# Tying the two readings of an attention bank to one engine, with corrected ScalarE costs and a new order, in a kernel whose order is planned

## The chip, the cores and the metric

The kernel runs on one core of a Trainium2 chip. The metric is device time in microseconds (us), the median of several executions.

Engines: PE is TensorE, ACT is ScalarE, DVE is VectorE, POOL is GpSimd, SP issues DMAs.

## The reference, cut to what matters

```python
x = A_x                                   # 2048 x 512, bf16
for _ in range(2):
    x = x + A(layernorm(x))               # linear attention, 32 heads of 16
    x = x + B(layernorm(x))               # gated MLP, 512 -> 1376 -> 512

def A(x):
    q, k, v = split_heads(x @ wqkv)
    phi = lambda t: concat(softmax(t @ w_phi), softmax(-(t @ w_phi)))
    kv, z = phi(k).T @ v, phi(k).sum(0)
    num, den = phi(q) @ kv, phi(q) @ z + 1e-6
    return merge_heads(num / den) @ wo
```

The kernel computes the attention quotient of 128 rows from three PSUM banks. Each bank holds numerators (here called N) and two denominator terms (DS) side by side.

## The kernel before

All work is recorded as a list of `Op`s. Each has an engine, a planned cost (how long it holds the engine, and how long until its result is ready), dependencies, buffers and a priority `due`. `plan()` is a list scheduler: it gives each engine, at each step, the waiting `Op` with the lowest `due`, and so fixes the order in which instructions are written. `DUE` holds one tuned number for each of the 2112 `Op`s. `PLACE` holds one bit for each `Op` that either of two engines could do.

The parts that the change touches:

```python
def act(n, sbuf=False):                    # planned ScalarE cost of n elements: (occupies, until ready)
    return (n / 1.2 + (275 if sbuf else 52), n / 1.2 + (385 if sbuf else 170))

def dve(n, rate=1, more=56):               # the same for VectorE
    t = n / rate / 0.96 + more
    return t, t + 98

def evac(eng, due, out_, in_, deps, takes, uses, name, cols=512):
    both = {"ACT": ("ACT", act(cols), lambda: nc.scalar.copy(...), False),
            "DVE": ("DVE", dve(cols), lambda: nc.vector.tensor_copy(...), False)}
    ...                                    # an Op with the other engine as alternative (alt)

def attend(l, t, due, eq, made, how):
    ...
    for k in range(3):
        ps = Buf(p_q)                      # one of three "q" banks
        ...                                # 3, 3 and 2 matmuls of 144 columns into it (L766)
        for out_, buf, lo, hi in ((ed, DS, DH, DH + 2), (en, N, 0, DH)):
            out_.append(evac("ACT", due, ...))      # two readings of the same bank
    ...                                    # DVE: m, den, reciprocal, w from DS; pr, o from N; projection

for o, w in zip([o for o in ops if o.alt], PLACE):
    if w == "1":
        o.swap()                           # to the other engine
order = arrange(ops)
...
for o in order:                            # in the plan's order; early gaps on TensorE get filler matmuls
    o.emit()
```

In `plan()` the two readings of a bank are independent: each needs only the matmuls. A bank is free when both have ended.

The softmax here doesn't subtract the row's maximum and nothing guards it: scores larger than these inputs give would overflow.

## Time and profile before

| | before |
|---|---|
| median time | 393.26 us on record; 392.62 us beside the kernel after |
| span in the trace | 390.9 us |
| PE busy | 382.7 us, 98% |
| matmuls | 2830 |
| split banks (N and DS on different engines) | 43 of 96 |

Busy time, first part of the page of before (time, share of the span, instructions):

```profile
PE 382.7 (98%) x2830; PEld 232.1 (59%) x2830; DVE 305.8 (78%) x783; ACT 223.0 (57%) x580; POOL 33.9 (9%) x36
```

98% is no measure of the room left, because matmuls overlap each other: one of 512 columns is on record as busy for 379 ns, and the next starts 216 ns after it. A busy PE may still be late. I therefore used the spacing of matmul starts. Its medians (216 ns for 512 columns, 109 for 256, 56 for 128, 62 for 144, and so on) come to 375.3 us over all matmuls. What lies above that is called **excess** below: 10.5 us.

Excess before, by stage: 4.64 us in the head (0 to 30 us), 0.05 in the rest of the key stage (to 58), 2.94 in the first attention stage (58 to 100), 0.06 to 243 us, 2.20 in the second attention stage (243 to 300), 0.58 after it. 3.37 us of it stands before attention matmuls.

The same stages in the windows view (busy us and number of instructions of each engine). DVE is nearly full (95%) in both attention stages:

```profile
core 0: us, PE busy (x) PEld busy (x) DVE busy (x) ACT busy (x) POOL busy (x), PEclk, DMA share, GB/s
...
58.00:100.00 42.00, 40.68 (x431) 31.26 (x430) 39.76 (x133) 30.79 (x91) 0.05 (x1) 1.00 0.20 39
100.00:243.00 143.00, 143.00 (x894) 80.05 (x893) 115.33 (x255) 74.55 (x186) 12.19 (x11) 1.00 0.16 32
243.00:300.00 57.00, 56.19 (x537) 39.83 (x535) 54.05 (x184) 37.61 (x109) 0.00 (x0) 1.00 0.24 49
```

From the waits view of before (who waited for whom: us in total, times, longest). L766 is the attention matmul, L596 an ACT copy, L597 a DVE copy:

```profile
PEld L766 <- issue: 2.7, 8, 0.6
...
ACT N L596 <- DVE DS L597: 1.2, 3, 0.5
...
ACT DS L596 <- DVE N L597: 1.0, 2, 0.6
...
DVE DS L597 <- ACT N L596: 0.8, 2, 0.6
...
PE q L766 <- ACT DS L596: 0.5, 1, 0.5
...
PE q L766 <- DVE DS L597: 0.4, 1, 0.4
...
PE q L766 <- DVE N L597: 0.3, 2, 0.2
```

N and DS do not use each other's data, and yet in this trace the second reading of a bank never starts before the first has ended (32 ns after it at the soonest) where the two are on different engines. The timeline of before shows how. A split bank (start us, duration us, engine, line): ACT reads DS from 291.62 to 291.82, and DVE starts on N at 291.86.

```profile
291.62 0.20 ACT L596 COPY DS<-q 128x48 f32<-128x48 f32 x1 [0.21 <-PE q L766]
291.86 0.56 DVE L597 CAST N<-q 128x384 bf16<-128x384 f32 x1
```

A bank that ACT reads twice: N starts at 107.94, before DS has ended.

```profile
107.86 0.19 ACT L596 COPY DS<-q 128x32 f32<-128x32 f32 x1 [0.95 <-PE q L766]
107.94 0.38 ACT L596 CAST N<-q 128x256 bf16<-128x256 f32 x1
```

Over all banks: the second reading of a split bank never starts sooner than 32 ns after the first has ended, and in 18 of 43 it starts within 50 ns of that end. In 27 of the 53 banks read by one engine, the second starts before the first has ended.

In this trace, a late matmul that takes a bank starts 51 to 54 ns after the last reading of that bank has ended, so each wait can be put down to its bank. ACT reads DS until 67.77 us:

```profile
67.54 0.23 ACT L596 COPY DS<-q 128x48 f32<-128x48 f32 x1
...
67.82 0.35 PE L766 MATMUL q<-R,Eq 128*128 128x144 bf16 x3 [0.51 <-ACT DS L596]
```

### The profile page before, as it was taken

The numbers are of one execution on the slowest core, as the hardware profiler recorded it, in microseconds if no ns is written. First come the engines' busy times: TensorE is split into PE (matmuls) and PEld (weight loads), VectorE is DVE, ScalarE is ACT, GpSimd is POOL, SyncE is SP. The second block draws the span as 40 slices with busy tenths as digits, with TensorE's granted clock in tenths as the row PEclk, the third lists the DMA queues.
The fourth block names the chain that finished last, engine by engine and source line by source line (L and its number), as shares of the span: only waits on it lengthen the run. The fifth ranks groups of instructions, "written<-read, shape, count | busy, mean of one in ns | idle before, by whom it ended". The sixth has DMA issues, their size and how long they took to land.

```text
span 390.9 us, 7625 instructions
## 1 busy us (share of the span) xinstructions
PE 382.7 (98%) x2830; PEld 232.1 (59%) x2830; DVE 305.8 (78%) x783; ACT 223.0 (57%) x580; POOL 33.9 (9%) x36
## 2 busy tenths in 40 slices
PE   8999998999999999999999999999999999999996
PEld 5455565878554644446676555586765445446865
DVE  6989979999998998649485797999999955333534
ACT  5999979746355535416726289985554350542311
POOL 0248420000100010204110100000000000000000
PEclk9999999999999999999999999999999999999999
DMA  8297540221431312020100100012242503101111
GB/s 246 71 217 208 152 138 1 48 58 35 81 70 40 56 27 55 18 43 17 27 15 20 27 3 1 2 32 59 55 88 68 82 15 82 27 0 49 32 31 42
DMA packets 60869, 22.83 MB, mean 58 GB/s; under 512 B 52672, under 2 KB 59808, under 8 KB 60832
## 3 DMA queue, kind: packets, MB, share of 16 engines
q1 hardware_dynamic: 60416, 21.95, 24.5%
q8 instruction: 22, 0.36, 0.4%
q10 hardware_dynamic: 416, 0.39, 0.4%
q14 instruction: 15, 0.12, 0.1%
HBM read 7.91 MB, written 2.10 MB: 26 GB/s over the span
## 4 chain that ended last, share of the span: by engine, by line
PE 74%; DVE 13%; ACT 7%; DMA 2%; issue 2%; SPq 1%; DVEq 0%; ACTq 0%
PE b L861 29%; PE b L894 18%; PE b L674 6%; PE b L680 6%; PE b L797 4%; PE q L711 3%; PE b L748 3%; ACT Eq L752 3%; ACT N L596 2%; PE b L837 2%; DVE pr L790 1%; PE q L766 1%; DVE N L597 1%; DVE X L801 1%; DMA xnTA<-xn 1%
## 5 line engine op out<-in xcount | busy, mean ns | idle before, releaser
L861 PE MATMUL b<-xnTB,wgu 128*128 128x128 bf16 (+2 forms) x1200 | 150.7, 279 | 0.0
L861 PEld LDWEIGHTS <-wgu 128*128 128x128 bf16 x1200 | 97.9, 98 | 43.0
L894 PE MATMUL b<-wd,hT 128*128 128x512 bf16 (+2 forms) x363 | 83.4, 373 | 0.0
L865 ACT ACTIVATE gu<-b 128x512 bf16<-128x512 f32 (+1 forms) x83 | 49.0, 594 | 51.7 <-PE b L861 46.9
L894 PEld LDWEIGHTS <-hT 128*128 128x128 bf16 (+1 forms) x363 | 34.4, 98 | 33.6
L869 DVE TENSOR_TENSOR hT<-gu 128x512 bf16<-128x512 bf16 (+1 forms) x83 | 34.3, 417 | 23.0 <-ACT gu L596 21.9
L694 POOL TENSOR_TENSOR phiK<-ek,sk 128x512 bf16<-128x512 bf16 x30 | 33.2, 1125 | 182.2 <-ACT sk L690 89.9
L596 ACT CAST gu<-b 128x512 bf16<-128x512 f32 (+1 forms) x55 | 32.3, 586 | 21.3 <-PE b L861 21.1
L685 DVE TENSOR_REDUCE sk<-ek 128x64 f32<-128x1024 bf16 x32 | 38.5, 1213 | 6.7 <-ACT ek L677 6.7
L677 ACT ACTIVATE ek<-b 128x512 bf16<-128x512 f32 x64 | 36.0, 610 | 10.3 <-PE b L674 10.0
L752 ACT ACTIVATE Eq<-b 128x512 bf16<-128x512 f32 x64 | 38.2, 659 | 2.4 <-PE b L748 2.4
L901 DVE SCALAR_TENSOR_TENSOR X<-b,rsB,X 128x512 bf16<-128x512 f32 (+1 forms) x33 | 23.8, 731 | 19.5 <-PE b L894 19.4
L596 ACT CAST N<-q 128x384 bf16<-128x384 f32 (+1 forms) x70 | 31.3, 487 | 8.3 <-PE q L766 4.3
L797 PE MATMUL b<-wo,oT 128*128 128x512 bf16 x128 | 32.7, 379 | 0.6 <-DMA oT<-o 0.4
L674 PE MATMUL b<-Wk,xnTA 128*128 128x512 bf16 x128 | 32.7, 379 | 0.1
L680 PE MATMUL b<-wv,xnTA 128*128 128x512 bf16 x128 | 32.4, 379 | 0.1
L748 PE MATMUL b<-xnTA,Wq 128*128 128x512 bf16 x128 | 31.7, 379 | 0.0
L766 PE MATMUL q<-R,Eq 128*128 128x144 bf16 x256 | 27.8, 226 | 1.5 <-ACT DS L596 0.5
L766 PEld LDWEIGHTS <-Eq 128*128 128x128 bf16 x256 | 20.2, 98 | 11.8 <-issue 2.7
L649 ACT ACTIVATE lnA<-mvA,eps 128x1 f32<-128x1 f32 x32 | 9.1, 307 | 28.9 <-DVE mvA L644 28.5
L597 DVE CAST gu<-b 128x512 bf16<-128x512 f32 (+1 forms) x28 | 18.6, 663 | 8.6 <-PE b L861 8.3
L694 DVE TENSOR_TENSOR phiK<-ek,sk 128x512 bf16<-128x512 bf16 x34 | 23.3, 717 | 1.4 <-ACT sk L690 1.2
(70 smaller groups left out, 413.3 us busy)
## 6 DMA issues: line engine op xcount, KB each, us to landing
out_dram<-X SPq DMA_DIRECT2D x15, 128.0 KB, 1.7
X<-in_A_x_dram SPq DMA_DIRECT2D x6, 256.0 KB, 3.7
wgu<-in_B_W_gate_dram SPq DMA_DIRECT2D x4, 344.0 KB, 4.2
wgu<-in_B_W_up_dram SPq DMA_DIRECT2D x4, 344.0 KB, 4.2
wd<-in_B_W_down_dram SPq DMA_DIRECT2D x5, 256.0 KB, 4.4
wv<-in_A_wqkv_dram SPq DMA_DIRECT2D x2, 256.0 KB, 4.4
wo<-in_A_wo_dram SPq DMA_DIRECT2D x4, 128.0 KB, 2.8
oT<-o SPq DMA_TRANSPOSE x28, 2.4
```

What stands on the lines that cost most here:

```text
L596: both = {"ACT": ("ACT", act(cols), lambda: nc.scalar.copy(out=out_(), in_=in_()), False), "DVE": ("DVE", dve(cols), lambda: nc.vector.ten ...
L674: k = op("PE", mm(4, 512), due, lambda: [nc.tensor.matmul(kp.t[:], lhsT=xnTA[c][:, b, cols], rhs=Wk2[:, b, :], start=(b == 0), stop=(b == ...
L680: v = op("PE", mm(4, 512), due_v, lambda: [nc.tensor.matmul(vp.t[:], lhsT=xnTA[c][:, b, cols], rhs=wv[:, b, :], start=(b == 0), stop=(b == ...
L685: a = op("DVE", SUM16, due, lambda: nc.vector.tensor_reduce(out=sk.t[:], in_=ek.t[:].rearrange("p s (h f) -> p (s h) f", f=DH), axis=AX.X, ...
L694: e.tensor_tensor(out=ph.t[:].rearrange("p s (h f) -> p (s h) f", f=DH)[:, lo:lo + n], in0=ek.t[:].rearrange("p s (h f) -> p (s h) f", f=D ...
L748: q = op("PE", mm(4, 512), due(c, b), lambda b=b, qp=qp: [nc.tensor.matmul(qp.t[:], lhsT=Wq2[:, m, b * P:(b + 1) * P], rhs=xnTA[c][:, m, : ...
L752: done.append(op("ACT", act(512), due(c, b), lambda b=b, s=s, qp=qp: nc.scalar.activation(out=Eq[c][:, b, s, :], in_=qp.t[:], func=AF.Exp, ...
L766: pe.append(op("PE", mm(len(groups), GE), due, lambda ps=ps, groups=groups: [nc.tensor.matmul(ps.t[:, n * GE:(n + 1) * GE], lhsT=Eq[c][:, ...
L797: a = op("PE", mm(4, 512), due + 3, lambda: [nc.tensor.matmul(yp.t[:], lhsT=oT.t[:, b, :], rhs=wo[:, b, :], start=(b == 0), stop=(b == NB ...
L861: nc.tensor.matmul(ps.t[:, q * W:(q + 1) * W], lhsT=wgu[:, s, b, g * P:(g + 1) * P], rhs=xT.t[:, b, 0:W], start=(b == 0), stop=(b == NB - 1))
L865: nc.scalar.activation(out=gu.t[:, 0, 0:cols], in_=gp.t[:, 0:cols], func=AF.Relu)
L894: nc.tensor.matmul(yp.t[:, 0:c1 - c0], lhsT=h.t[:m, f * W + i * P:f * W + (i + 1) * P], rhs=wd[:m, f, c0:c1], start=(f == 0), stop=(f == N ...
```

## The change

Its intent: a bank's two readings stay on one engine, so that neither has to wait for another engine's reading of the bank, as in the 43 split banks above (32 ns or more from end to start); ScalarE's planned costs follow the spacing of instruction ends in a trace; priorities and engine choices are annealed anew for that plan (searched by many small random changes, of which those are kept that make the plan end sooner).

```diff
     def swap(self):
+        if self.twin:
+            self.twin.swap()
 ...
-    return (n / 1.2 + (275 if sbuf else 52), n / 1.2 + (385 if sbuf else 170))
+    return (n / 1.2 + (275 if sbuf else 64), n / 1.2 + (385 if sbuf else 170))
 ...
-            a = op("ACT", (210, 310), due, ...Ln of the key sums
+            a = op("ACT", (150, 265), due, ...
-            a = op("ACT", (110, 220), due, ...Exp of the key sums
+            a = op("ACT", (145, 262), due, ...
 ...
-            for out_, buf, lo, hi in ((ed, DS, DH, DH + 2), (en, N, 0, DH)):
+            for out_, buf, lo, hi in ((en, N, 0, DH), (ed, DS, DH, DH + 2)):
 ...
+            ed[-1].twin = en[-1]
 ...
-    for o, w in zip([o for o in ops if o.alt], PLACE):
+    tied = {o.twin for o in ops if o.twin}
+    for o, w in zip([o for o in ops if o.alt and o not in tied], PLACE):
 ... (PLACE: 301 new bits for 397; DUE: 2112 new numbers)
```

## The prediction

> **What bounds the kernel.** TensorE. The page gives PE 98% busy at full clock. Busy hides waits, so I took the start-to-start spacing of the 2830 matmul records. The medians (216 ns for 512 columns, 109 for 256, 82 for 192, 62 for 144, 56 for 128) summed over all matmuls give 375.3 us of the 390.9 us span. The rest: 1.2 us before the first matmul, 10.5 us of excess spacing, 3.8 us after the last matmul starts. Of the excess, 4.6 us lies in the first 30 us (1.7 us is the warm-up matmuls' double spacing); 3.3 us lies before attention matmuls (L766) waiting for a "q" bank; the rest is mostly waits for transposed tiles. From 100 to 243 us there is practically none. DVE and ACT matter only where they release banks late.
>
> **What the change does.**
> 1. Each of 96 attention banks has two evacuations, N and DS; 43 banks are split between ACT and DVE. The second reading of a split bank never starts sooner than 32 ns after the first ends; in 18 of 43 it starts within 50 ns of it, with 3.0 us of engine idle time before those. In banks read by one engine, 27 of 53 second readings start before the first has ended. [...] The kernel's plan treats the two as independent, so a split bank comes free later than planned. The change leaves no split banks.
> 2. It corrects planned ScalarE costs. End-to-end spacing of back-to-back instructions: 488 ns for 512 elements (plan 479, now 491), 383 for 384 (372, now 384), 102 for 48 (92, now 104), 145 for both small Ln and Exp of the key sums (210 and 110, now 150 and 145).
> 3. The order is annealed anew. Counted from the built program: 9 phi products (717 ns each on DVE, 1125 on POOL) go to POOL; 10 more 512-wide gu copies (682 against 599 ns) go from ACT to DVE. TensorE's instructions are the same but for 14 filler matmuls instead of 11: +0.65 us in the first 15 us, partly in stalls.
>
> **On the critical path.** Only the excess spacing can shrink. The bank waits (3.3 us) should fall to about 1 us. Of the other waits after 50 us (2.3 us) perhaps a third goes; new ones will appear where the order puts attention between other blocks. Head: about zero, fillers included. Net about -2 us. Without any stall after the head the kernel would still be near 387.5 us, so over 2% (385.4) is out of reach.
>
> **Prediction:** 391.2 us, 8 in 10 between 389.2 and 393.2. Faster by over 2%: 0.02; within 2%: 0.95; slower by over 2%: 0.03.
>
> **What would show it.** Excess spacing falls from 10.5 to about 8.5 us, mostly in 58 to 100 us and 243 to 300 us; attention-bank waits fall under 1.5 us; in the waits view no ACT N or DS behind a DVE reading, or the reverse; DVE's phi count is 25, POOL's 39.
>
> **What would make it wrong.** One engine for both readings may lengthen a bank's hold where that engine has a backlog; DVE is full from 60 to 160 and 250 to 310 us. POOL's phi products [...] may lengthen DVE instructions. A head 2 us longer would eat the gain..

## More of the kernel before

All executions compared here are fast, with a granted TensorE clock of 0.998 to 1.0.

Waits that the plan did not foresee show as lateness against it: by 320 us the ACT and DVE instructions of before start 5.54 us later than planned (the table is under "Where runs leave their plan").

## The result, and the profile after

The kernel after takes 390.54 us (median of 6, 390.05 to 391.35); before takes 392.62 us in the same rounds. The ratio of the fast runs is 0.9945, 95% interval 0.993 to 0.996. A ratio is always the mean time of one kernel's fast runs over that of the other's of the same rounds, so it is not quite the ratio of the medians quoted here. The gain is clear of noise and under 2%.

```profile
PE 379.0 (98%) x2789; PEld 231.2 (60%) x2833; DVE 309.5 (80%) x785; ACT 217.7 (56%) x569; POOL 43.5 (11%) x45
```

This trace lacks 44 matmul records: there are 2833 weight loads and 2789 matmuls. Each lost record of a 512-column matmul shows up as a false excess of 216 ns. I took 44 times 216 ns out of all sums below, and did the same for the other traces that lack some.

The span, term by term (us):

| | before | after | difference |
|---|---|---|---|
| before the first matmul | 1.19 | 1.34 | +0.15 |
| all matmuls at their undisturbed spacing | 375.3 | 375.9 | +0.65 (3 more fillers) |
| excess: head, 0 to 30 us | 4.64 | 3.08 | -1.56 |
| excess: 30 to 58 | 0.05 | 0.51 | +0.46 |
| excess: first attention stage, 58 to 100 | 2.94 | 3.06 | +0.12 |
| excess: 100 to 243 | 0.06 | 0.23 | +0.17 |
| excess: second attention stage, 243 to 300 | 2.20 | 0.86 | -1.34 |
| excess: 300 to the end | 0.58 | 0.05 | -0.53 |
| from the last matmul's start to the end | 3.81 | 3.39 | -0.43 |

The terms add up to within 0.2 us of the two spans. Of the excess, what stands before attention matmuls fell from 3.37 to 1.81 us. By bank, the 1.4 us at split banks are gone, and the 1.9 us at banks read by one engine are still 1.7.

One profile is one execution. The profile of e4 (below) is of a kernel that differs from after only in fillers of the head; its excess in the first attention stage is 2.1 us where after has 3.1, while the 1.8 us before attention matmuls are the same. A difference of 1 us in a stage between two profiles can therefore be chance.

The windows view of after in the same stages:

```profile
58.00:100.00 42.00, 39.91 (x407) 29.36 (x410) 39.87 (x125) 27.57 (x82) 0.00 (x0) 1.00 0.18 36
100.00:243.00 143.00, 142.16 (x894) 81.37 (x909) 110.67 (x251) 79.48 (x197) 22.02 (x19) 1.00 0.17 33
243.00:300.00 57.00, 56.44 (x523) 39.57 (x528) 52.61 (x166) 34.45 (x98) 0.00 (x0) 1.00 0.25 52
```

From the waits view of after (L733 is the attention matmul, L765 the output projection; L563 and L564 are the ACT and DVE copies). No N or DS waits for the other engine's reading of its bank any more. After the start, TensorE's longest single wait in this trace is for a transposed tile (oT, at 80 us); the trace of e4, in the same order, does not have it:

```profile
PEld L765 <- DMA oT<-o: 1.5, 2, 1.2
...
PEld L733 <- issue: 1.4, 3, 0.6
...
PE b L765 <- DMA oT<-o: 0.8, 1, 0.8
...
PE q L733 <- ACT N L563: 0.5, 1, 0.5
...
PE q L733 <- DVE DS L564: 0.4, 1, 0.4
```

So the time came out as predicted, but only part of the gain lies where the prediction put it: the sum is right partly by luck. The experiments ask what the tie, the costs and the new order are each worth.

### The profile page after: what moved, and what is told of

Its sections match the earlier page's. It is cut to its first block, busy times and chain, and to the rows that moved or that the text cites. A ratio compares the mean times of both kernels' runs of the same rounds, so it can differ in the third digit from the quotient of the medians.

```text
span 388.6 us, 7611 instructions
## 1 busy us (share of the span) xinstructions
PE 379.0 (98%) x2789; PEld 231.2 (60%) x2833; DVE 309.5 (80%) x785; ACT 217.7 (56%) x569; POOL 43.5 (11%) x45
## 4 chain that ended last, share of the span: by engine, by line
PE 82%; DVE 7%; ACT 4%; DMA 3%; SPq 2%; issue 2%; DVEq 0%; ACTq 0%
PE b L829 32%; PE b L862 19%; PE b L765 7%; PE b L641 5%; PE b L647 5%; PE b L715 4%; PE q L678 3%; PE b L805 3%; PE q L733 3%; ACT Eq L719 2%; DMA xnTA<-xn 1%; SPq L486 1%; DMA oT<-o 1%; ACT ek L644 1%; DVE N L564 1%
## 5 line engine op out<-in xcount | busy, mean ns | idle before, releaser
L862 PE MATMUL b<-wd,hT 128*128 128x512 bf16 (+2 forms) x348 | 82.1, 372 | 0.8
L661 POOL TENSOR_TENSOR phiK<-ek,sk 128x512 bf16<-128x512 bf16 x39 | 42.8, 1114 | 193.4 <-ACT sk L657 145.3
L652 DVE TENSOR_REDUCE sk<-ek 128x64 f32<-128x1024 bf16 x32 | 38.6, 1209 | 8.1 <-ACT ek L644 8.0
L563 ACT CAST gu<-b 128x512 bf16<-128x512 f32 (+1 forms) x46 | 26.1, 566 | 31.7 <-PE b L829 31.4
L719 ACT ACTIVATE Eq<-b 128x512 bf16<-128x512 f32 x64 | 35.4, 623 | 4.7 <-PE b L715 4.5
L564 DVE CAST gu<-b 128x512 bf16<-128x512 f32 (+1 forms) x37 | 25.0, 677 | 13.2 <-PE b L829 13.0
L765 PE MATMUL b<-wo,oT 128*128 128x512 bf16 x121 | 31.7, 379 | 1.2 <-DMA oT<-o 0.8
L563 ACT CAST N<-q 128x384 bf16<-128x384 f32 (+1 forms) x63 | 27.9, 461 | 8.4 <-DVE pr L758 3.2
L715 PE MATMUL b<-xnTA,Wq 128*128 128x512 bf16 x125 | 30.7, 379 | 0.2
L733 PE MATMUL q<-R,Eq 128*128 128x144 bf16 x256 | 26.8, 226 | 1.1 <-ACT N L563 0.5
L733 PEld LDWEIGHTS <-Eq 128*128 128x128 bf16 x256 | 19.9, 98 | 11.3 <-issue 1.4
L769 DVE TENSOR_TENSOR X<-X,b 128x512 bf16<-128x512 bf16 x32 | 21.5, 676 | 2.3 <-PE b L765 2.2
L610 DVE BATCH_NORM_STATS2 bstA<-X 128x6 f32<-128x512 bf16 x32 | 21.2, 681 | 1.8 <-DMA X<-in_A_x_dram 1.6
```

The source lines that it names most:

```text
L563: both = {"ACT": ("ACT", act(cols), lambda: nc.scalar.copy(out=out_(), in_=in_()), False), "DVE": ("DVE", dve(cols), lambda: nc.vector.ten ...
L661: e.tensor_tensor(out=ph.t[:].rearrange("p s (h f) -> p (s h) f", f=DH)[:, lo:lo + n], in0=ek.t[:].rearrange("p s (h f) -> p (s h) f", f=D ...
L715: q = op("PE", mm(4, 512), due(c, b), lambda b=b, qp=qp: [nc.tensor.matmul(qp.t[:], lhsT=Wq2[:, m, b * P:(b + 1) * P], rhs=xnTA[c][:, m, : ...
L719: done.append(op("ACT", act(512), due(c, b), lambda b=b, s=s, qp=qp: nc.scalar.activation(out=Eq[c][:, b, s, :], in_=qp.t[:], func=AF.Exp, ...
L733: pe.append(op("PE", mm(len(groups), GE), due, lambda ps=ps, groups=groups: [nc.tensor.matmul(ps.t[:, n * GE:(n + 1) * GE], lhsT=Eq[c][:, ...
L765: a = op("PE", mm(4, 512), due + 3, lambda: [nc.tensor.matmul(yp.t[:], lhsT=oT.t[:, b, :], rhs=wo[:, b, :], start=(b == 0), stop=(b == NB ...
```

## The experiments

Theory A: the split readings, which the plan does not know of, made the attention-bank waits, and the tie removes them. Rival B: the gain is the new order. Later theories: C (a truer plan pays), D (any further annealing pays), E (orders of one quality scatter by some us), F (one engine's costs must not be raised without the other's).

All 12 kernels gave correct results. Ratios are to before, in the same rounds.

| run | what | median us | ratio (95% interval) | excess | before attention matmuls |
|---|---|---|---|---|---|
| before | | 392.62 | 1 | 10.5 | 3.4 |
| after | | 390.54 | 0.9945 (0.993 to 0.996) | 7.8 | 1.8 |
| e1 | old order, tied | 391.86 | 0.9984 (0.9964 to 1.0003) | 9.2 | 2.8 |
| e2 | new order, 43 split | 393.68 | 1.0017 (0.9999 to 1.0034) | no fast profile | |
| e3 | new order, 96 split | 396.96 | 1.0111 (1.0094 to 1.0128) | 14.3 | 8.1 |
| e4 | after, no later fillers | 390.45 | 0.9940 (0.9922 to 0.9958) | 8.0 | 1.8 |
| e5 | annealed: neither | 390.84 | 0.9956 (0.9937 to 0.9976) | 9.3 | 2.8 |
| e6 | annealed: costs only | 394.42 | 1.0046 (1.0027 to 1.0065) | 12.4 | 1.9 |
| e7 | annealed: tie only | 390.70 | 0.9948 (0.9926 to 0.9970) | 9.0 | 1.6 |
| e8 | annealed: tie and costs | 392.83 | 1.0007 (0.9987 to 1.0027) | 11.0 | 1.0 |
| e9 | all costs, tied | 390.19 | 0.9944 (0.9930 to 0.9957) | 7.4 | 0.5 |
| e11 | all costs, tied, other order | 389.89 | 0.9943 (0.9926 to 0.9961) | 7.5 | 0.3 |
| e10 | all costs, untied | 393.72 | 1.0029 (1.0016 to 1.0043) | no fast profile | |
| e12 | e10 again | 394.32 | 1.0035 (1.0012 to 1.0058) | 12.0 | 2.1 |

### The tie alone, in the old order (e1)

The plan and its order stay; only the engine of 43 DS readings is changed after planning.

```diff
     order = arrange(ops)
+    for d, n in [p for ed, en in banks for p in zip(ed, en)]:
+        if d.eng != n.eng:
+            d.swap()
```

> The kernel before, its order, slots and plan unchanged, only the 43 split banks' DS reading moved to the engine of the N reading. Theory A (split readings, unknown to the plan, made the attention-bank waits): 1.0 to 1.8 us faster than before (ratio about 0.996), waits before attention matmuls down from 3.3 to under 2 us, no N or DS waiting behind the other engine's reading. Rival B (the gain is the new order; the tie alone does nothing where the order was made without it): within 0.4 us of before, bank waits about 3 us.

Measured: ratio 0.9984, about 0.6 us faster, with an interval that includes no gain. No N or DS waits behind the other engine any more, but 2.8 us are still lost before attention matmuls. The 1.4 us at split banks are gone; the waits at banks read by one engine rose from 1.9 to 2.75 us, which fits an order that has no place there for the readings that were moved. In the second attention stage the excess fell from 2.20 to 1.10 us; in the first it rose from 2.94 to 3.14. Theory A had asked for 1.0 us and bank waits under 2 us; by the waits this is nearer to B. The tie alone, in an order not made for it, was not shown to gain.

### Splitting again, in the new order (e2, e3)

The kernel after in its order; after planning, DS of the 43 banks that were split before (e2), or of all 96 (e3), goes to the other engine.

```diff
     order = arrange(ops)
+    for (d, n), w in zip([p for ed, en in banks for p in zip(ed, en)], SPLIT):
+        if w == "1":                       # e3: always
+            d.twin = None
+            d.swap()
```

> The kernel after, its order unchanged, but the DS reading of the same 43 banks that were split before goes to the other engine again. Theory A: 1 to 2 us slower than after (391.5 to 392.5), bank waits rise from 1.8 to about 3 us. Rival B: within 0.4 us of after.

> The kernel after, its order unchanged, DS of all 96 banks moved to the engine that does not read N. Theory A: about twice the loss of the run with 43, 2.5 to 4 us slower than after, bank waits 4 us or more. Rival B: within 0.6 us of after.

Measured beside e4, which is after without its later fillers and equal to it within noise: e2 1.0017/0.994 = 1.008, about 3 us slower; e3 1.0111/0.994 = 1.017, about 6.7 us slower. Both lose more than theory A expected (1 to 2 and 2.5 to 4 us), and the loss about doubles with the number of split banks. e2's profile fell into a slow execution (572.82 us at a granted clock of 0.656, left out). From the waits view of e3 (three of its four such lines; ACT and DVE sit idle for the other's reading of the same bank):

```profile
ACT N L563 <- DVE DS L564: 13.0, 18, 2.2
...
ACT DS L563 <- DVE N L564: 6.2, 10, 1.6
...
DVE N L564 <- ACT DS L563: 3.3, 4, 2.0
```

With the fourth they make 23.1 us of engine idle time, and TensorE loses 8.1 us before attention matmuls, against 1.8. The timeline of e3 shows one case: DVE ends its DS readings at 88.56, ACT, idle for 1.44 us, starts on N at 88.59, and TensorE waits for ACT.

```profile
88.26 0.30 DVE L564 COPY DS<-q 128x48 f32<-128x48 f32 x2
...
88.59 0.75 ACT L563 CAST N<-q 128x256 bf16<-128x256 f32 x2 [1.44 <-DVE DS L564]
89.02 0.35 PE L734 MATMUL q<-R,Eq 128*128 128x144 bf16 x3 [0.67 <-ACT N L563]
```

Put down to banks as above, 5.7 of the 8.1 us are at banks whose second reading had just waited for its turn. At the other 2.3 us the last reading was late for another reason, such as work before it on its engine. In e3, then, taking turns on a bank delayed its release, and TensorE waited for it (the 5.7 us). This does not say that the tie is worth 3 us in the change, because this order was made for tied banks, and e3 also moves some load from ACT to DVE.

### The fillers (e4)

```diff
-        free, filling = None, True
+        free, filling = None, False
```

> The kernel after without the 6 filler matmuls that follow the first 8. Theory A1 (they mostly sit where TensorE waits anyway): 0 to 0.5 us faster than after, same clock. Rival: each costs its 216 ns, 1.3 us faster. Rival: they keep the clock up, and without them the early matmuls are slower and the time is longer by over 0.5 us.

Measured: 390.45 us, the same as after. The six later fillers cost nothing: without them the excess in the head is 4.21 instead of 3.08 us, and six fillers are worth 6 x 216 ns = 1.3 us. They fill time in which TensorE waits anyway. For the rival that fillers keep the clock up, the trace of after has only this: the first eight matmuls, of 512 columns, start 398 to 427 ns apart, and those from 7.1 us on mostly 216. Without the six later fillers the granted clock was 0.999 to 1.0 in all six executions and the time did not change, so that rival was not shown.

### Neither, one or both, annealed anew (e5 to e8)

The old priorities fit the old costs only: with the new ScalarE costs and the old `DUE`, `plan()` ends in a deadlock of buffers, and so do the old costs with the new `DUE`. Each part therefore had to be annealed for itself. I started all four from the order of before and made 500,000 steps each (move one priority next to that of a neighbour in time, or flip an engine choice; keep it if the plan's own end falls, with a small falling temperature). The edits are the tie and the cost lines of the change, with new `DUE` and `PLACE` each time.

```diff
 e5: neither part              (43 banks split)
 e6: 52 -> 64, (210, 310) -> (150, 265), (110, 220) -> (145, 262)    (48 split)
 e7: ed[-1].twin = en[-1]      (none split)
 e8: both
```

> Control. The kernel before with neither tie nor new costs, its order and engine choices annealed further by me (500,000 steps from its own order; the plan's own end falls by 0.4 us). Theory C (a truer plan is what pays): no gain over before, 391.9 to 393.9, bank waits 3 us or more. Rival D (any further annealing pays): 0.4 us or more faster.

> The kernel before with only the new ScalarE costs in the plan, splits still allowed and unknown to the plan, annealed in the same way from the same order. Theory C: 0.3 to 1 us faster than before, bank waits still near 3 us with N or DS waiting behind the other engine. Theory A (the tie is all): no gain. Rival D: as the control.

> The kernel with the tie but the old ScalarE costs in the plan, annealed in the same way from the same order. Theory C: 0.7 to 1.5 us faster than before, bank waits about 2 us. Theory A: the whole gain, about 2 us. Rival D: as the control.

> Tie and new ScalarE costs together, annealed in the same way from the order of before: the change done again with another order. Theory C and A: 1.5 to 2.5 us faster than before, bank waits under 2 us. Rival E (the gain of after is the luck of one order): no better than the control.

These were the misses. The control gained as much as the change does (0.9956), against theory C. The costs alone made the kernel slower (1.0046), against C as well. The tie alone gained 0.9948, more than C allowed, though not clearly more than the control. Both together, in my order, gave no gain (1.0007), where the change itself gives 0.9945. So one order tells little: the same change with two orders differs by about 2.4 us.

Two things still hold in these runs. First, with either set of costs the tied kernel is no slower than the untied one: 0.9948 against 0.9956 (within noise), and 1.0007 against 1.0046. Second, in my orders the new ScalarE costs push work to VectorE. The page of e6:

```profile
PE 380.6 (97%) x2788; PEld 230.6 (59%) x2832; DVE 320.1 (81%) x811; ACT 215.6 (55%) x548; POOL 38.2 (10%) x40
```

DVE is busy for 320.1 us in e6 and 319.5 in e8, against 314.2 in e5 and 314.7 in e7. In after, whose order was made with the same new costs, it is only 309.5, so the costs alone do not force this. Not all of the difference is more work, either. In these traces some DVE instructions that read only SBUF take longer while POOL makes a phi product: a phi product (the last step of phi of the keys) takes about 680 ns on DVE alone and up to 1546 beside one of POOL's. DVE statistics, key sums and copies from PSUM do not change; in the trace of after their medians, alone and beside a phi product of POOL, are 683 and 680 ns (statistics of the key stages' input), 1210 and 1209 (key sums), 694 and 683 (copies of v from PSUM). This adds 5.7 us to DVE's busy time in e5, 8.1 in e6, 7.6 in e7 and 7.4 in e8.

DVE's planned costs are also too low: the ends of back-to-back 512-element products are 600 ns apart in the trace of after, where the plan has 589; centring takes 262 where the plan has 240.

### All costs corrected, with and without the tie (e9, e10, e11, e12)

```diff
-def dve(n, rate=1, more=56):
+def dve(n, rate=1, more=67):
-    return t, t + 98
+    return t, t + 87
-STATS = (592, 692)
-SUM16 = (1140, 1225)
-CENTRE, SCALE = (240, 350), (315, 410)
+STATS = (600, 690)
+SUM16 = (1125, 1212)
+CENTRE, SCALE = (262, 350), (322, 410)
 ... (and a few ns on the small ones; ScalarE as in after; e10 and e12 without the tie, 52 banks split)
```

> Tie and new ScalarE costs as in after, and VectorE costs raised as well to the end-to-end spacing in the trace (copies and products 11 ns more, centring 22, scaling 7, statistics 8; key sums 15 less), order annealed further by me from that of after. Theory F (raising ScalarE's planned times alone pushes work to VectorE, whose planned times are still too low; with both true the plan holds): 387 to 389.5 us, faster than after by 1 us or more, VectorE busy under 312 us, attention-bank waits under 1.5 us. Rival E (any order of this quality measures 390.5 give or take 2 us): 389 to 393 us.

> The same ScalarE and VectorE costs without the tie, annealed for the same number of steps from the order of before; splits are allowed and unknown to the plan. Theory F with A (the tie is worth 1 to 1.5 us in the two attention stages): 1 to 2.5 us slower than the tied run beside it, bank waits near 3 us, second attention stage with about 1.5 us more excess spacing. Rival: within 0.6 us of the tied run.

> As the tied run with all costs, another seed of the same annealing (plan end 0.3 us later): tells the scatter between orders of one plan. Theory F: within 0.8 us of the other seed. Rival E: may differ by 2 us.

> The kernel of the untied run with all costs again[...]. Theory A with F: about 393.7 us again; against the tied run of all costs (excess spacing 7.4 us, of it 0.5 us bank waits) at least 1.5 us of the 3.3 us difference is waits before attention matmuls, with N or DS waiting behind the other engine, and the first and second attention stage hold most of it. Rival E (luck of the order): bank waits under 1.5 us, and the difference lies in the key stages or in the head.

Each had 1,700,000 steps; the tied ones started from the order of after, the untied one from that of before. That is one flaw of this comparison. The others are that there is one untied order only, and that e9 and e11 share their first 700,000 steps and part only after that, so that they tell less of the scatter than two orders made apart would.

Measured: e9 and e11 differ by 0.0001 in their ratios, as theory F expected, but at 390.19 us e9 misses the 389.5 us that F had asked for at most. The untied kernel is 1.0029/0.9944 = 1.0085 times e9, about 3.3 us slower, in the same rounds. e10's profile fell into a slow execution (2289.71 us, with a granted clock of 1.0 on record), so it was run again as e12. Against e9, e12 has 4.6 us more excess: 1.7 us before attention matmuls; by stage 1.7 us more in the first attention stage and 0.8 in the second, but also 1.6 in the key stage, 0.8 from 100 to 243 us and 0.6 after 300, with 0.8 less in the head. The bank waits are what theory A with F asked for (1.5 us or more); that the attention stages hold most of the difference is true by a little only, and the rest is the order. The waits view of e12 (L490 and L491 are its ACT and DVE copies) has the cross-engine waits back, 4.9 us in all:

```profile
DVE DS L491 <- ACT N L490: 2.3, 7, 0.6
...
ACT DS L490 <- DVE N L491: 1.5, 4, 0.6
...
ACT N L490 <- DVE DS L491: 0.8, 3, 0.4
...
DVE N L491 <- ACT DS L490: 0.3, 1, 0.3
```

In e9's waits view the whole of what its attention matmuls (L662) wait for on the TensorE side is one line:

```profile
PEld L662 <- issue: 0.2, 1, 0.2
```

e9 is not faster than after: 390.19 and 390.54 us come from different rounds, and the ratios are equal. What it saves in attention it loses in the head (4.32 against 3.08 us) and in the key stage (1.05 against 0.51). No version was found that clearly beats after.

### Where runs leave their plan

`plan()` gives each `Op` a start. I matched these with the starts in the trace, for all ACT and DVE instructions, and took the median lateness of those that the plan starts in the 5 us after the time named. What counts is how it grows across a stage (us late):

| | at 50 us | at 80 | at 240 | at 320 | growth, 1st attention | growth, 2nd attention |
|---|---|---|---|---|---|---|
| before, untied | 1.06 | 2.62 | 2.83 | 5.54 | 1.56 | 2.71 |
| e5, untied | 0.77 | 1.63 | 2.90 | 4.59 | 0.86 | 1.69 |
| e6, untied | 2.96 | 4.37 | 6.34 | 8.04 | 1.41 | 1.70 |
| e12, untied | 4.00 | 4.70 | 6.09 | 7.52 | 0.70 | 1.43 |
| after, tied | 0.86 | 2.09 | 2.44 | 2.81 | 1.23 | 0.37 |
| e7, tied | 2.14 | 2.95 | 3.74 | 4.32 | 0.81 | 0.58 |
| e8, tied | 3.44 | 3.67 | 5.97 | 6.42 | 0.23 | 0.45 |
| e9, tied | 2.48 | 2.50 | 3.05 | 3.19 | 0.02 | 0.14 |
| e11, tied | 1.84 | 1.85 | 2.85 | 3.03 | 0.01 | 0.18 |
| e4, tied, order of after | 0.73 | 1.03 | 1.37 | 1.65 | 0.30 | 0.28 |
| e1, tied after planning | 0.24 | 1.93 | 2.21 | 4.30 | 1.69 | 2.09 |
| e3, 96 split after planning | 0.95 | 3.92 | 5.68 | 9.18 | 2.97 | 3.50 |

In the second attention stage the four untied orders lose 1.4 to 2.7 us against their plans and the five tied ones 0.1 to 0.6, whatever the costs: 1.88 against 0.34 on average, 1.5 us. The plans themselves end at almost the same time (384.7 us on average untied, 384.9 tied), and TensorE's own excess in that stage agrees: 0.9 to 2.3 us untied, 0.1 to 0.9 tied. The last two rows belong to neither group, because they run another choice of engines than they were planned with: e1 shows that tying banks in an order planned without the tie keeps most of the loss (2.09 of 2.71 us).

The first attention stage is no such evidence: after loses 1.23 us there and e4, in the same order, 0.30, and with a window of 5 us to both sides the figure of e12 is 1.27 instead of 0.70. The small figures of e9 and e11 are thus not shown to come from VectorE's costs. The lateness at 50 us, before any attention, has nothing to do with banks. It varies from 0.7 to 4.0 us between the runs that kept to the plan's choice of engines, and it is largest in the three slowest of them (e6, e8 and e12).

## Why the prediction was right, point by point

- **What bounds the kernel: right.** Only excess could shrink, and no run came near the 2% that the prediction called out of reach: the best was 389.89 us against the 387.5 us named as the floor.
- **The size: right, partly by luck.** 2.0 us predicted, 2.1 measured. The bank waits gave less than predicted, and the head and the end gave about 1.2 us that was not predicted.
- **The counts: right.** DVE makes 25 of the phi products and POOL 39. The worry that POOL's products lengthen DVE instructions was right in kind and cost little here. All DVE instructions that took over 60 ns longer than their like ran beside a phi product of POOL: together 1.7 us more before and 2.1 after. In after it is mainly two of the products that normalise x (xn), of 1147 and 1209 ns, where those alone take 404; DVE's phi products went from 717 to 694 ns on average.
- **Attention-bank waits: right in direction, too large in size.** Predicted to fall from 3.3 to about 1 us; they fell to 1.8. The cross-engine waits did vanish, and with them the 1.4 us at split banks. But the prediction took the whole 3.3 us for the work of splits: 1.9 us were at banks read by one engine, which a tie does not address, and waits of that kind are still 1.7 us. In the first attention stage they are waits for ACT and DVE backlog: the reading that released the bank came with no idle time of its engine before it.
- **Other waits after 30 us: not settled.** The prediction let a third of 2.3 us go. Excess after 30 us that is not before attention matmuls was 5.83 - 3.37 = 2.5 us and is 4.71 - 1.81 = 2.9 in after, of which 0.92 us is a new wait for a transposed tile at 80 us. In e4, the same order, that wait is missing and the figure is about 2.0. So these waits differ between executions by more than what was predicted.
- **The head: missed.** Predicted about zero, fillers included. Its excess fell by 1.56 us, with 0.65 us of new fillers and a 0.15 us later start: about 0.8 us net. e4 shows that fillers are free there. Another 0.43 us came after the last matmul and was not foreseen. It goes with the order and not with the tie: e5, untied, has the same 3.39 us there, and e1, tied in the old order, the old 3.81.
- **"These are truer": true, but the implied gain was not shown.** The new ScalarE costs match the trace of before (491 ns planned for 512 elements, 488 between ends). Alone they made the kernel slower in my order (e6). By the planned costs my orders with them shift about 5 us of work to DVE, whose costs were still too low. That this is why e6 and e8 are slow agrees with e9, where DVE's costs were corrected too, but e9 also started elsewhere and was annealed longer, so it is argued, not isolated.

What the gain consists of: the plan of after ends later than that of before (385.7 against 384.8 us by the plan's own reckoning), but the run falls 2.8 us behind its plan instead of 5.5 by 320 us. 2.3 us of that difference is the second attention stage (2.71 against 0.37), where tied orders differ from untied ones in all nine cases. I take the tie to be worth about 1.5 us there, in an order made for it; this is inferred from nine orders, and no single run isolates it. On TensorE, what is shown is that 1.4 us of waits at split banks went away; the rest of the gain lies in the head and the end, and goes with the new order; no run tests why. The tie is not the only way to 390.5 us: the control e5 gets there untied.

**Still open:** why orders of almost equal plan lose 0.7 to 4.0 us by the end of the key stage. Waits for transposed key inputs (xnTA) recur there: 0.45 us in after, 0.76 in e9, 1.24 in e8. And how large the scatter between untied orders with all costs is, since one was run.

## What to carry to other kernels

In five traces with 282 split banks, two engines that read one PSUM bank took turns, although they read different columns: no second reading started sooner than 31 ns after the first had ended. A hand-made plan for such banks has to know that, or keep a bank's readings on one engine. A change that comes with a newly annealed order can't be credited to its idea before a control has been annealed as long without it: here the control gained as much. Before a wait is credited to a cause, look up which buffer each wait was for: here only 1.4 of 3.4 us belonged to the banks that the change was about. That planned costs of all engines should be corrected together, or the planner moves work to the engine whose costs are still too low, is what e6 and e8 suggest; after is a counterexample, and no run isolates it.

## What else the traces show for such a plan

- What the turns cost: in the trace of before the second reading of a split bank starts 32 to 34 ns after the first has ended, in 17 of the 18 tightest cases, while one engine's second reading may start up to 313 ns before its first has ended. A matmul that waits for the bank starts 51 to 54 ns after the last reading.
- A plan needs two figures for an instruction: the trace of after has 488 ns between ends of back-to-back ScalarE instructions of 512 elements from PSUM (586 to 597 from start to end), and 600 ns for VectorE copies (684 from start to end).
- This kernel loads weights for every matmul (2830 of each in before), and its matmuls of 128 and 512 columns still start 56 and 216 ns apart.
- Whole executions of kernels of 393 us took 572.82, 1423.44 and 2289.71 us. The granted clock on record was 0.656 in the first, but 1.0 in the other two, so the record alone does not find them. The spacing of matmuls does: 512-column matmuls start 360 ns apart in the trace of the first and 1278 ns in that of the third, instead of 216. The second left no trace.
- Lost matmul records can be counted from the weight loads: 44 of 2833 are missing in after, all of 512 columns and never two within 50 matmuls.
